# A feed-forward in four 64x64 quadrants of the TensorE array, with the lower rows one product behind the upper

## The chip, the cores and the metric

The kernel runs on one core of one Trainium2 chip. The metric is device time of one execution in microseconds (us), median of several runs. The span that a profile gives, from the first to the last instruction, is about 1.9 us shorter than the timed run (392.3 against 394.16 us before).

## The reference

Sigmoid attention, then a feed-forward with SiLU. Cut to what matters:

```python
q, k, v: (8 batches, 12 heads, 448, 64)         # float32
scores = q @ k.T / sqrt(64) - log(448)
attn   = sigmoid(scores) @ v                    # (8, 12, 448, 64)
x      = attn.transpose(0, 2, 1, 3).reshape(3584, 768)
h      = x @ w_in                               # w_in (768, 2048)
g      = h * sigmoid(h)
out    = g @ w_out                              # w_out (2048, 768)
```

## The kernel before

The kernel works in float16. A unit is 4 heads of one batch, so there are 24 units. The attention products S (scores) and V (values) contract over 64 and give 64 rows. They already run in the four 64x64 quadrants of the array, four matmuls at a time (in the trace three of a group start 3 to 4 ns behind the one before, and the V groups of 448 columns follow each other every 189 ns):

```python
def v_matmuls(pt, n, slots, N):
    for c in range(NCH):
        for h in range(2):              # rows 0-63 or 64-127 of the array
            for j in range(2):          # columns 0-63 or 64-127
                ck = NCH * j + c
                nc.tensor.matmul(
                    pt[64 * j : 64 * j + 64, h, :N],
                    v16[n % NV][64 * h : 64 * h + 64, j, c * D : (c + 1) * D],
                    at[64 * h : 64 * h + 64, slots[ck // 2], ck % 2, :N],
                    start=(c == 0), stop=(c == NCH - 1), skip_group_check=True,
                )
```

The feed-forward uses the whole 128x128 array. Its first product (G1) is this; the second (G2) has the same form, 384 columns wide, in a seven-product scheme of which only the count matters here (14 pairs of output blocks, 7 products of 8 matmuls each):

```python
def piece(self):                        # G1: one or two blocks of 128 hidden units
    # ... (cut)
    def go(z, fc):
        for cc in range(NCC):           # 6 blocks of the contraction
            nc.tensor.matmul(
                bank[:, z * N : z * N + N], wi[:, cc, fc * P : (fc + 1) * P], x[:, cc, c0:c1],
                start=(cc == 0 and z == 0), stop=(cc == NCC - 1), skip_group_check=True,
            )
    # ... (cut)
```

For the first two batches G1 is done in two "narrow" parts, of 256 and of 192 columns, so that it can begin early; later batches use 448 columns. Attention steps are set between feed-forward products. A plan in Python decides the order; in the compiled program the order on each engine is fixed. The inputs are loaded by GpSimd-issued DMA, 224 KB per load of queries, keys or values of one unit, up to 384 KB for `w_in` and 768 KB for `w_out` (the figures in the code are the plan's own estimates, and no argument here rests on them):

```python
def load(key, deps, fn, nd, size):
    first = [("issue", pl.loads)] if pl.loads else []
    pl.loads += 1
    pl.op("POOL", 650, key, deps + first, fn, nbytes=nd / 16 * (21 + 0.0368 * size))
```

## Time and profile before

| | before |
|---|---|
| median time | 394.16 us (3 runs) |
| span in the profile | 392.3 us |
| TensorE busy | 98% |
| changes of form, 76 to 329 us | 144, each about 98 ns |
| TensorE instructions in the program, waits not counted | 7,448 |

The list of what TensorE waited for (us in total, times, longest), kernel before:

```profile
PE gm L355 <- DMA xq<-in_q_dram: 1.4, 1, 1.4
PE gm L841 <- DVE warm L195: 1.2, 1, 1.2
PE gm L346 <- DMA xk<-in_k_dram: 0.8, 1, 0.8
PE gm L579 <- DVE xt L830: 0.3, 1, 0.3
PE att L407 <- ACT at L812: 0.2, 1, 0.2
```

The timeline of TensorE, kernel before (start in us, duration in us, group). Eighteen matmuls of the whole array are 18 x 189.2 ns = 3.41 us by their spacing, and two groups of four quadrants 0.38 us. A round (131.46 to 135.47) takes 4.01 us, so two changes of form cost 0.22 us.

```profile
131.46 0.57 PE L407 MATMUL att<-qT,kT 64*64 64x448 f16 x8
131.96 3.58 PE L579 MATMUL gm<-xt,wi 128*128 128x448 f16 x18
135.47 0.57 PE L407 MATMUL att<-qT,kT 64*64 64x448 f16 x8
```

### The profile page before, as it was taken

How to read it: one execution, taken by the hardware profiler on the slowest of the kernel's cores; microseconds unless marked ns; L12 is line 12 of the kernel's file. 1: busy time of each engine (PE TensorE's matmuls, PEld its weight loads, DVE VectorE, ACT ScalarE, POOL GpSimd, SP SyncE). 2: the span in 40 equal slices, each digit the busy share in tenths (PEclk: the TensorE clock that was granted, in tenths of full speed). 3: DMA queues.
4: the chain of work that ended last, by engine and by line, in shares of the span. 5: the costliest groups of instructions: out<-in, count | busy, mean ns of one | idle time of the engine just before them, and what ended most of it. 6: DMA issues, size and time to landing. Idle time of an engine off the chain costs nothing.

```text
span 392.3 us, 8872 instructions
## 1 busy us (share of the span) xinstructions
PE 383.0 (98%) x3723; PEld 210.2 (54%) x3723; DVE 199.7 (51%) x326; ACT 222.7 (57%) x332; POOL 65.0 (17%) x97
## 2 busy tenths in 40 slices
PE   6999999999999999999999999999999999999995
PEld 2567777775454455444454444444554445555562
DVE  1444788545455444554546345545554445554552
ACT  1876787487556855567645875686554772144110
POOL 9655322502222021020120120000000000000000
PEclk8999999999999999999999999999999999999998
DMA  7999999999999786993487877632023001320333
GB/s 105 199 209 203 210 208 203 164 143 145 158 192 196 105 137 116 179 165 74 73 149 174 149 123 99 107 71 52 21 62 82 0 2 34 82 48 2 70 81 91
DMA packets 80599, 45.93 MB, mean 117 GB/s; under 512 B 50608, under 2 KB 79792, under 8 KB 80560
## 3 DMA queue, kind: packets, MB, share of 16 engines
q0 software_dynamic: 25008, 22.81, 39.9%
q1 hardware_dynamic: 55552, 22.56, 31.9%
q8 instruction: 29, 0.48, 0.5%
q14 instruction: 10, 0.08, 0.1%
HBM read 45.61 MB, written 11.01 MB: 144 GB/s over the span
## 4 chain that ended last, share of the span: by engine, by line
PE 93%; DVE 2%; DMA 1%; ACT 1%; issue 1%; POOL 0%; ACTq 0%; POOLq 0%; DVEq 0%
PE gm L579 37%; PE gm L665 34%; PE att L407 11%; PE att L419 8%; PE gm L355 1%; DMA xq<-in_q_dram 1%; PE gm L856 1%; ACT at L812 1%; PE gm L346 1%; DVE gs L272 0%; DVE gt L542 0%; DVE xt L830 0%; ACT sg L537 0%; DVE qT L376 0%; DVE wo L272 0%
## 5 line engine op out<-in xcount | busy, mean ns | idle before, releaser
L579 PE MATMUL gm<-xt,wi 128*128 128x448 f16 (+2 forms) x960 | 158.4, 316 | 0.4 <-DVE xt L830 0.3
L451 ACT ACTIVATE at<-att 128x896 f16<-128x896 f32 x126 | 109.6, 916 | 52.5 <-PE att L407 52.5
L542 DVE TENSOR_TENSOR gt<-gm,sg 128x448 f16<-128x448 f32 (+2 forms) x128 | 79.8, 624 | 90.7 <-ACT sg L537 90.5
L579 PEld LDWEIGHTS <-wi 128*128 128x128 f16 x960 | 86.0, 98 | 66.4 <-issue 14.9
L537 ACT ACTIVATE sg<-gm 128x448 f16<-128x448 f32 (+2 forms) x128 | 70.1, 548 | 53.7 <-PE gm L579 49.0
L679 DVE SCALAR_TENSOR_TENSOR us<-gm,us 128x384 f32<-128x384 f32 x70 | 38.7, 553 | 46.5 <-PE gm L665 31.4
L665 PE MATMUL gm<-wo,gt 128*128 128x384 f16 x336 | 61.3, 327 | 0.0
L665 PEld LDWEIGHTS <-gt 128*128 128x128 f16 x448 | 42.0, 98 | 34.2 <-issue 7.9
L407 PE MATMUL att<-qT,kT 64*64 64x448 f16 (+2 forms) x840 | 53.8, 325 | 0.6 <-ACT at L812 0.2
L812 ACT ACTIVATE at<-att 128x1024 f16<-128x1024 f32 (+3 forms) x48 | 37.7, 826 | 15.2 <-PE att L407 15.0
L665 PEld LDWEIGHTS <-gs 128*128 128x128 f16 x336 | 31.6, 98 | 25.4 <-issue 5.7
L235 POOL DMA_DIRECT2D v<-in_v_dram x24 | 17.4, 725 | 138.3 <-PE att L407 122.5
L665 PE MATMUL gm<-so,gs 128*128 128x384 f16 x224 | 40.3, 327 | 0.0
L419 PE MATMUL att<-at,v 64*64 64x448 f16 (+2 forms) x840 | 37.6, 314 | 0.1
L686 ACT ACTIVATE us<-gm 128x384 f32<-128x384 f32 x28 | 13.8, 493 | 40.7 <-PE gm L665 39.6
L407 PEld LDWEIGHTS <-kT 64*64 64x64 f16 x840 | 17.7, 106 | 27.8 <-issue 23.2
L419 PEld LDWEIGHTS <-v 64*64 64x64 f16 x840 | 21.2, 106 | 13.6 <-issue 6.8
L461 DVE TENSOR_SCALAR xt<-att 128x896 f16<-128x896 f32 x18 | 19.6, 1091 | 11.4 <-PE att L419 11.4
L224 POOL DMA_DIRECT2D xq<-in_q_dram x27 | 19.8, 735 | 15.4 <-issue 5.8
L665 PE MATMUL gm<-wo,gs 128*128 128x384 f16 x112 | 21.0, 326 | 0.0
L665 PE MATMUL gm<-so,gt 128*128 128x384 f16 x112 | 21.0, 326 | 0.0
L215 POOL DMA_DIRECT2D xk<-in_k_dram x24 | 17.5, 727 | 15.8 <-PE gm L346 8.9
(32 smaller groups left out, 114.6 us busy)
## 6 DMA issues: line engine op xcount, KB each, us to landing
out_dram<-us SPq DMA_DIRECT2D x112, 96.0 KB, 2.2
xk<-in_k_dram POOLq DMA_DIRECT2D x24, 224.0 KB, 7.2
v<-in_v_dram POOLq DMA_DIRECT2D x24, 224.0 KB, 6.6
xq<-in_q_dram POOLq DMA_DIRECT2D x21, 224.0 KB, 8.5
wo<-in_moe_w_out_dram POOLq DMA_DIRECT2D x4, 768.0 KB, 15.3
wi<-in_moe_w_in_dram POOLq DMA_DIRECT2D x8, 192.0 KB, 7.5
wi<-in_moe_w_in_dram POOLq DMA_DIRECT2D x4, 384.0 KB, 9.7
qT<-xq SPq DMA_TRANSPOSE x32, 3.8
```

Source lines behind the costliest of these rows:

```text
L215: lambda: nc.gpsimd.dma_start(xk[n % NX].rearrange("p (j c) -> p j c", j=2), src(k, b, g)),
L224: lambda: nc.gpsimd.dma_start(xq[n % NX][:, D : D + 2 * S].rearrange("p (j c) -> p j c", j=2)[:, :, lo:hi], src(q, b, g)[:, :, lo:hi],),
L407: nc.tensor.matmul(pt[64 * h : 64 * h + 64, r, lo : lo + (c1 - c0) * D], kT[n % NTR][64 * r : 64 * r + 64, i, 64 * h : 64 * h + 64], qT[n ...
L419: nc.tensor.matmul(pt[64 * j : 64 * j + 64, h, :N], v16[n % NV][64 * h : 64 * h + 64, j, c * D : (c + 1) * D], at[64 * h : 64 * h + 64, sl ...
L451: lambda: nc.scalar.activation(at[:, sl], pt[:, :, :S], AF.Sigmoid, bias=NEG_LOG_S, scale=QKSCALE),
L461: lambda: nc.vector.tensor_scalar_mul(x[:, 2 * g : 2 * g + 2, :], pt[:, :, :S], SX), prio=-2,
L537: lambda: nc.scalar.activation(t[:, :ncol], src_, AF.Sigmoid, scale=ISX), prio=0,
L542: lambda: nc.vector.tensor_tensor(o, src_.rearrange("p (a t) -> p a t", a=nb), t[:, :ncol].rearrange("p (a t) -> p a t", a=nb), ALU.mult),
L579: nc.tensor.matmul(bank[:, z * N : z * N + N], wi[:, cc, fc * P : (fc + 1) * P], x[:, cc, c0:c1], start=(cc == 0 and z == 0), stop=(cc == ...
L665: nc.tensor.matmul(bank[:, :HE], lhs[:, c, :], rhs[:, c, :], start=first and c == 0, stop=(c == HFC - 1), skip_group_check=True,)
L679: lambda: nc.vector.scalar_tensor_tensor(o, bank[:, :HE], ISX, u, ALU.mult, ALU.add), prio=-2,
L812: lambda: nc.scalar.activation(at[:, base : base + m, :, :N], src_, AF.Sigmoid, bias=NEG_LOG_S, scale=QKSCALE),
```

## The change

The intent: run everything in quadrants, so that the array never changes its form. Each feed-forward matmul becomes four. The upper rows (h = 0) and the lower rows (h = 1) of one product add into the same bank of PSUM, where this kernel's matmuls write their results. The plan keeps the two from being in it at once, which I took to be needed. So the lower rows work on a product whose upper rows ended at least 450 ns earlier, and a semaphore makes TensorE wait for its own earlier matmul. Transposes become quadrant matmuls against the identity, and all PSUM tiles become single banks, so attention evictions are split in two. The core of the diff (the rest, on the plan's order, banks and evictions, is cut):

```diff
-            def go(z, fc):
-                for cc in range(NCC):
-                    nc.tensor.matmul(
-                        bank[:, z * N : z * N + N], wi[:, cc, fc * P : (fc + 1) * P], x[:, cc, c0:c1],
-                        start=(cc == 0 and z == 0), stop=(cc == NCC - 1), skip_group_check=True,
-                    )
+            def mm(h, c):
+                z, cc = divmod(c, NCC)
+                f0 = fcs[z] * P
+                return [
+                    nc.tensor.matmul(
+                        bank[64 * j : 64 * j + 64, z * N : z * N + N],
+                        wi[64 * h : 64 * h + 64, cc, f0 + 64 * j : f0 + 64 * j + 64],
+                        x[64 * h : 64 * h + 64, cc, c0:c1],
+                        start=(c == 0 and h == 0), stop=(h == 1 and cc == NCC - 1), skip_group_check=True,
+                    )
+                    for j in range(2)
+                ]
...
+    def lower_ready():
+        if not fifo:
+            return False
+        q, c = fifo[0]
+        return c > 0 or (q.left is not None and pl.t >= q.left + 450.0)
+
+    def lane_step(p=None, c=0):
+        low = fifo.popleft() if lower_ready() else None
+        ...
+        def go():
+            if p:
+                p.last = p.mm(0, c)[-1]
+            if low:
+                if low[1] == 0:
+                    wait = nc.tensor.nop()
+                    left = low[0].last
+                ins = low[0].mm(1, low[1])
+                if low[1] == 0:
+                    for a_, b_ in ((wait, left), (ins[0], wait)):
+                        tc.add_manual_dep(
+                            a_.ins, b_.ins.name,
+                            mybir.DependencyInfo(mybir.DependencyClass.Sync, mybir.DependencyReason.DATA),
+                            reason="the upper rows have left the bank",
+                        )
```

G2 is changed in the same way, with 384 columns. The compiled program has 18,338 TensorE instructions instead of 7,448, and 226 waits of TensorE on itself.

## The prediction

> **What bounds the kernel now.** TensorE. The page shows PE busy 98% of the 392.3 us span, the waits of TensorE sum to about 4 us (all at the start), and the chain of waits is 93% PE. So what fills that busy time? From the starts of successive matmuls (timeline): 128x448 products follow each other every 189 ns; four 64x64 matmuls of 448 columns start 3 to 4 ns apart, and such a group also takes 189 ns; 384 columns take 162.5 ns. Feed-forward work at these rates is 273 us (960 + 784 matmuls), attention 64 us. The rest:

> - Changes between the 128x128 and the 64x64 form. From 76 to 329 us I count 144, each adding about 98 ns to the normal spacing: 14.1 us. Before 76 us there are 98 more, with 13 us (some of it waits for data). [...]
> - Transposes: 56 + 112 groups at 56 ns, 9.4 us. Filler matmuls on zeros, start and tail: about 5 us each.

> **What the change removes.** All mode changes (about 23 us clean), and about 6 us of transposes (112 groups of four small matmuls, estimated at 29 ns each, instead of 168 at 56).

> **What it adds.** Four times as many feed-forward matmuls of a quarter of the size: the same array work if both halves are full. The build order shows where they aren't: 58 steps with the upper half alone, 58 with the lower alone (14 us, half of it wasted: 7 us), and some 500 steps that pair a 448- with a 384-column product and last as long as the wider (7 us wasted). By counts times measured spacing, feed-forward is 287 us instead of 273. ScalarE evictions are split by bank: 916 ns becomes 2 x 548, +23 us, about 66% busy overall, but near 90% before 76 us, where it and the loads (DMA full from 10 to 68 us) hold back part of the gain.

> **Rate of the quadrants.** The attention products already run four quadrants at full rate, with weight loads of 106 ns hidden (even at 192 columns: 82.5 ns per group). I expect the feed-forward to do the same. [...]

> **The wait on itself.** 226 waits, one per product, each placed at least 450 ns after the upper rows' last matmul. That matmul lasts 349 ns in the trace, so the semaphore should already be there: under 25 ns each, mostly nothing.

> **Sum.** First stage ends near 70 us instead of 76. After it: 255.5 us feed-forward, 47.7 us attention, 5 us tail, 2 us of stalls: span about 380, time about 381.5 us (timed runs lie 1.9 us over the span).

> Predicted 381.5 us, 80% range 373 to 391. Faster by over 2%: 0.69; within 2%: 0.23; slower: 0.08.

> **Right if** groups start every 189 and 162 ns throughout, no 98 ns steps remain, waits of TensorE on TensorE sum to a few us, ScalarE is near 250 us busy, and attention visits cost just their 189 ns per group.

> **Wrong if** TensorE cannot be fed: 18,338 instructions instead of 7,448 mean about 20 ns each, and no stretch before shows more than one matmul per 50 ns for long; then groups are over 189 ns apart and time may rise far above 394. Or if each self-wait costs 100 ns or more (+20 us). Or if late loads, ScalarE or full banks show as new waits of TensorE in the first 80 us.

The 7 us for steps with one half alone are counted from the build order that has the lag. The 29 ns for a group of four transposes are an estimate that can be worked out from the trace of before: 82.5 ns at 192 columns and 189.2 ns at 448 are 26.7 ns for each 64 columns and 2.5 ns beside. In the changed kernel they took 31 to 32 ns.

## More of the kernel before

From the page of the kernel before: its first lines, three rows of the table in 40 slices of 9.8 us (busy tenths; PEclk is the granted clock of TensorE in tenths; DMA is the mean busy share of the 16 DMA engines), and the row of the DMA queue that brings instructions (packets, MB, share of the 16 engines' span).

```profile
span 392.3 us, 8872 instructions
...
PE 383.0 (98%) x3723; PEld 210.2 (54%) x3723; DVE 199.7 (51%) x326; ACT 222.7 (57%) x332; POOL 65.0 (17%) x97
...
PE   6999999999999999999999999999999999999995
...
PEclk8999999999999999999999999999999999999998
DMA  7999999999999786993487877632023001320333
...
q8 instruction: 29, 0.48, 0.5%
```

TensorE is full all the way (98%), its clock is up (0.993 on average; at half only from 7.8 to 11.2 us), and DMA is full from the second slice to the thirteenth (10 to 127 us, 186 GB/s). The line of q8 looks harmless, and the prediction did not use it. Read with the count after the change (below), it says that TensorE's program comes in packets of 0.48 MB / 29 = 16 KB while the kernel runs (29 packets for 7,448 instructions, and 72 for 18,338 after the change: one for about 256).

## The result, and the profile after

The changed kernel is slower: median 415.65 us (414.08 to 417.07, 4 runs) against 393.99 us (4 runs). The ratio is 1.0547, with a 95% interval of 1.0496 to 1.0599. Ratios are computed as the mean time of one kernel's runs over that of the other's in the same rounds, so they are not quite the ratio of the medians quoted. Results are correct in this and in every run below.

The same parts of the page, kernel after (a slice is 10.4 us):

```profile
span 415.2 us, 20334 instructions
...
PE 376.3 (91%) x9168; PEld 322.7 (78%) x9168; DVE 203.6 (49%) x376; ACT 234.6 (56%) x506; POOL 65.0 (16%) x97
...
PE   7769667885699989999999999999999999999995
...
PEclk9996888999899999999999999999999999999999
DMA  8999995399449994969868999654413101220234
...
q8 instruction: 72, 1.18, 1.2%
```

TensorE has holes in the first third and is as full as before afterwards. In the same stretch its clock drops: the trace shows it at half for 20.4 us in five spells between 32 and 114 us, one of 6.8 us and four of 3.4 us. In them a group of 256 columns mostly takes 213 ns instead of 109, and one of 192 columns 160 ns instead of 83. The list of TensorE's waits, kernel after (all lines of over 0.4 us):

```profile
PE ps L666 <- issue: 25.0, 15, 3.0
PE ps L765 <- issue: 2.4, 3, 0.9
PE ps L451 <- issue: 1.4, 1, 1.4
PE ps L493 <- DVE qT L465: 1.3, 4, 0.6
PE ps L947 <- DVE warm L195: 1.2, 1, 1.2
PE ps L451 <- DMA xk<-in_k_dram: 0.9, 1, 0.9
PE ps L493 <- DVE xt L936: 0.6, 2, 0.3
PE ps L666 <- DVE xt L936: 0.5, 1, 0.5
```

"issue" means that the engine waited for nothing that the profile shows: no semaphore, no buffer, no other engine. It is 29 us in 19 gaps, and there was none before. The timeline of TensorE shows two such gaps whole, kernel after:

```profile
40.42 0.56 PE L666 MATMUL ps<-xt,wi 64*64 64x256 f16 x10
42.80 2.05 PE L666 MATMUL ps<-xt,wi 64*64 64x256 f16 x67 [1.83 <-issue]
...
45.98 0.52 PE L666 MATMUL ps<-xt,wi 64*64 64x256 f16 x12
48.76 1.58 PE L666 MATMUL ps<-xt,wi 64*64 64x256 f16 x34 [2.26 <-issue]
```

```
kernel  block  entered  pause just  fetch in it     fetch   next block  length of
        at no. at, us   before, us  starts after    took    entered at  the block
before   1217   41.50     0.11        2.07 us       0.97     48.48        6.98
before   1473   48.48     0.08        2.79          0.97     55.29        6.81
before   4033  161.01     0.00        0.53          0.89    177.15       16.14
after     961   24.72     1.39        3.58          0.89     30.78        6.06
after    1473   36.77     0.03        3.63          0.95     42.80        6.03
after    1729   42.80     2.10        3.67          0.94     48.76        5.96
after    1985   48.76     2.53        4.19          0.94     55.38        6.62
after    2241   55.38     2.16        3.75          0.97     61.55        6.17
after    2753   67.80     1.85        1.64          0.95     71.63        3.83
after    9409  207.68     0.15        1.54          0.89    213.28        5.60
```

(The pause is start to start, so it includes a normal spacing. Block 4033 has a second fetch, 14.65 us after its start.) While DMA is full (205 GB/s from 20 to 67 us), a block of the changed kernel lasts about 6.1 us (5.90 to 6.62): about 3.7 us until the fetch begins, 0.95 us for the fetch, and about 1.4 us from its landing to the next block's first instruction (1.25 to 1.60). The kernel before took 6.27 us or more for every block, and it has no pause. (In its quiet stretch this link is not seen: a fetch begun at 208.57 us landed 0.87 us after the next block had been entered, without a pause. So how far ahead of TensorE a fetch must land is not settled for that stretch.) The changed kernel has 18,338 instructions for 7,448, at the same spacing of the groups, and would use up a block of narrow products in an estimated 2.6 to 3.5 us: 32 groups (four weight loads and four matmuls each) at the measured 82.5 to 109 ns. After 67 us the fetch starts sooner (1.64 and 1.05 us after entry) and the blocks get shorter at once (3.83 and 3.59 us). But they do not get short enough: from 67.8 to 71.6 us DMA moved only 6 GB/s, and the block still lasted 3.83 us, with a pause of 1.16 us behind it. So narrow products in quadrants used up a block too soon here even beside a nearly idle DMA; beside a full one the pauses are more and longer (eight of 1.4 to 2.9 us between 18 and 68 us).

The pauses of over 0.3 us at block ends sum to 34.6 us in the changed kernel (20 of them; one after 200 us, at 399 us, where DMA is light; that one is not explained) and to nothing in the kernel before. Where the loss lies is seen from the start of the last narrow G1 matmul: at 90.4 us before, at 118.8 us after. From there to the end the kernel before takes 301.9 us and the changed one 296.4 us. All of the loss, and more, falls before that point: 28.4 us, and the pauses before it sum to 28.6 us. (That the two agree so closely is partly chance: the half-clock spells fell there too, and the quadrant transposes saved an estimated 5.8 us, from 168 groups at 56 ns before and 112 at 32 ns after.)

The speed of the quadrants is as predicted. From 202 to 398 us, 4,399 times a matmul and the fourth one behind it were compared: the spacing is 188 to 190 ns or 162 to 163 ns in most of them, and over 200 ns in 88.

### The profile page after: what moved, and what is told of

It reads as the page before. It is cut to its first block, busy times and chain, and to the rows that moved or that the text cites. A ratio compares the mean times of both kernels' runs of the same rounds, so it can differ in the third digit from the quotient of the medians.

```text
span 415.2 us, 20334 instructions
## 1 busy us (share of the span) xinstructions
PE 376.3 (91%) x9168; PEld 322.7 (78%) x9168; DVE 203.6 (49%) x376; ACT 234.6 (56%) x506; POOL 65.0 (16%) x97
## 4 chain that ended last, share of the span: by engine, by line
PE 88%; issue 7%; DVE 2%; DMA 1%; POOL 0%; ACT 0%; POOLq 0%
PE ps L666 39%; PE ps L765 31%; PE ps L493 8%; PE ps L505 8%; PE ps L451 1%; DMA xq<-in_q_dram 1%; DVE kT L465 1%; DVE qT L465 1%; PE ps L947 0%; DVE so L272 0%; DVE xt L936 0%; ACT at L914 0%; DVE wo L272 0%; POOL xk L215 0%; DVE us L779 0%
## 5 line engine op out<-in xcount | busy, mean ns | idle before, releaser
L666 PE MATMUL ps<-xt,wi 64*64 64x448 f16 (+2 forms) x3840 | 229.6, 323 | 25.5 <-issue 25.0
L666 PEld LDWEIGHTS <-wi 64*64 64x64 f16 x3840 | 161.4, 112 | 46.0 <-issue 30.3
L536 ACT ACTIVATE at<-ps 128x448 f16<-128x448 f32 x252 | 122.4, 547 | 46.0 <-PE ps L493 41.4
L615 DVE TENSOR_TENSOR gt<-ps,sg 128x448 f16<-128x448 f32 (+2 forms) x128 | 78.1, 622 | 97.1 <-ACT sg L610 96.8
L610 ACT ACTIVATE sg<-ps 128x448 f16<-128x448 f32 (+2 forms) x128 | 69.7, 550 | 75.3 <-PE ps L666 71.3
L765 PE MATMUL ps<-wo,gt 64*64 64x384 f16 x1344 | 109.8, 323 | 0.0
L765 PEld LDWEIGHTS <-gt 64*64 64x64 f16 x1792 | 98.6, 107 | 8.7 <-issue 0.6
L765 PEld LDWEIGHTS <-gs 64*64 64x64 f16 x1344 | 79.2, 107 | 11.8 <-issue 3.7
L765 PE MATMUL ps<-so,gs 64*64 64x384 f16 x896 | 84.7, 323 | 1.5 <-issue 1.5
L493 PE MATMUL ps<-qT,kT 64*64 64x448 f16 (+2 forms) x840 | 80.4, 320 | 2.4 <-DVE qT L465 1.3
L786 ACT ACTIVATE us<-ps 128x384 f32<-128x384 f32 x28 | 13.8, 495 | 32.4 <-PE ps L765 30.9
## 6 DMA issues: line engine op xcount, KB each, us to landing
wi<-in_moe_w_in_dram POOLq DMA_DIRECT2D x4, 384.0 KB, 9.6
```

The source lines that it names most:

```text
L493: nc.tensor.matmul(pt[r][64 * h : 64 * h + 64, lo : lo + (c1 - c0) * D], kT[n % NTR][64 * r : 64 * r + 64, i, 64 * h : 64 * h + 64], qT[n ...
L536: lambda r=r: nc.scalar.activation(at[:, sl, r], pt[r][:, :S], AF.Sigmoid, bias=NEG_LOG_S, scale=QKSCALE),
L610: lambda: nc.scalar.activation(t[:, :ncol], src_, AF.Sigmoid, scale=ISX), prio=0,
L615: lambda: nc.vector.tensor_tensor(o, src_.rearrange("p (a t) -> p a t", a=nb), t[:, :ncol].rearrange("p (a t) -> p a t", a=nb), ALU.mult),
L666: nc.tensor.matmul(bank[64 * j : 64 * j + 64, z * N : z * N + N], wi[64 * h : 64 * h + 64, cc, f0 + 64 * j : f0 + 64 * j + 64], x[64 * h : ...
L765: nc.tensor.matmul(bank[64 * j : 64 * j + 64, :HE], lhs[64 * h : 64 * h + 64, c, 64 * j : 64 * j + 64], rhs[64 * h : 64 * h + 64, c, :], s ...
```

## The experiments

Theory A: TensorE runs out of instructions at block ends, because the fetch of the next block is held up while DMA is full of data loads. Theory B: the waits of TensorE on itself cost the time. Both were suppositions until the runs; that the fetch queues behind the data, as some expectations put it, was not shown (few3). Other rivals were that a quadrant feed-forward is slow in itself, and that late buffers hold it.

### lag900: twice the lag

```diff
-        return c > 0 or (q.left is not None and pl.t >= q.left + 450.0)
+        return c > 0 or (q.left is not None and pl.t >= q.left + 900.0)
...
-            pl.t = max(pl.t, q.left + 450.0)
+            pl.t = max(pl.t, q.left + 900.0)
```

> The changed kernel with the lower rows at least 900 ns behind the end of the upper rows instead of 450. Theory A (instruction blocks: TensorE runs out of instructions at every 256th, because the fetch of the next 16 KB block queues behind the data loads): nothing changes in the count of instructions or the loads, so 411 to 420 us, with pauses at the same instruction numbers 193 + 256k and a sum of 28 to 36 us. Theory B (the waits of TensorE on itself cost the time): with the semaphore long there, the lost 20 to 30 us come back, under 400 us.

Measured: 418.58 us (415.82 to 421.98, 4 runs), ratio to before 1.0576 (1.0524 to 1.0629). Pauses at 193 + 256k sum to 34.0 us, and in the stretch of full DMA blocks last 5.75 to 6.20 us. The edit also changes the order of the plan. Theory B expected under 400 us, and it falls.

### cols: twice the instructions in the kernel before, no quadrant feed-forward

In the kernel before, each feed-forward matmul of 128 columns is cut into its left and its right half. The array runs the two side by side, as the time shows: one after the other they would double the 273 us of feed-forward work, and the runs took 396.19 and 399.84 us. The edit:

```diff
                 for cc in range(NCC):
-                    nc.tensor.matmul(
-                        bank[:, z * N : z * N + N], wi[:, cc, fc * P : (fc + 1) * P], x[:, cc, c0:c1],
-                        start=(cc == 0 and z == 0), stop=(cc == NCC - 1), skip_group_check=True,
-                    )
+                    for j in range(2):
+                        nc.tensor.matmul(
+                            bank[64 * j : 64 * j + 64, z * N : z * N + N], wi[:, cc, fc * P + 64 * j : fc * P + 64 * j + 64], x[:, cc, c0:c1],
+                            start=(cc == 0 and z == 0), stop=(cc == NCC - 1), skip_group_check=True,
+                        )
```

(G2 in the same way.)

> The kernel before, with each feed-forward matmul of 128 columns cut in two of 64 (left and right half of the array at once): twice its instructions, the same array time, no lag and no wait of TensorE on itself, all changes of form kept. Theory A: in the first 76 us a block of 256 instructions would last about 5.1 us, under the 6.0 to 6.3 us that a fetch takes there, so pauses of about 1 us appear at every 256th instruction; 5 to 12 us are added before 76 us, little after (400 to 407 us). Theory B: 394 us, no such pauses.

Measured: 396.19 and 399.84 us; ratio 1.0079 (1.0011 to 1.0147). Five pauses of 0.4 to 2.1 us, 4.4 us together, stand at numbers 1729, 1985, 2241, 2497 and 3265, which are 193 + 256k again; the blocks between lasted 5.92 to 6.19 us. There is neither a lag nor a self-wait in this kernel, and its clock was not at half from 3.9 to 396.4 us, so these pauses came without a dropped clock. The loss is smaller than I expected, since only five blocks were used up before the next had come, and at 2% it counts as the same time; but the signature is there without any part of the lag scheme.

### traffic and before_traffic: more DMA where it was light

Both kernels get 48 more loads into spare tiles that nothing reads, four behind each of the loads of units 12 to 23. TensorE's program stays the same, instruction for instruction, in both.

```diff
+    spare = [sb(f"spare{i}", [2, S], F16) for i in range(4)]
+    extra = [0]
+
+    def load_spare(n):
+        b, g = divmod(n, NQ)
+        z = extra[0] % 4
+        extra[0] += 1
+        nc.gpsimd.dma_start(spare[z], src(v, b, g))
...
         load_v(n)
+        if n >= 12:
+            for z in range(4):
+                pl.op("POOL", 650, ("spare", n, z), [("v", n)], lambda n=n: load_spare(n))
```

> The changed kernel with 48 more loads of values into spare tiles that nothing reads, four behind each of the loads of units 12 to 23: DMA stays busy where it was light. Instructions of TensorE are the same. Theory A: after 200 us, where the changed kernel had two pauses at block ends, new ones of 0.3 to 2 us appear at instruction numbers 193 + 256k, wherever DMA is full; 5 to 20 us longer, with DMA share over 0.9 there. Theory B: no new pauses; only waits for late data, if any, which would be at the attention products and not at block ends.

> The kernel before with the same 48 extra loads. Theory A: here a block of 256 instructions lasts 14 to 16 us after 100 us, far over what a fetch takes even in a full queue, so no pause at block ends; the time stays within 394 to 400 us, and what is added is waits for late data. If instead TensorE is 30 us or more late here too, the extra loads hurt by themselves and the run with them says nothing of the fetch.

Measured, one look each: the changed kernel with the loads takes 455.56 us, the kernel before with the same loads 395.11 us (before alone in those rounds: medians 394.54 and 394.31 us). From the page of the changed kernel with the extra loads (a slice is 11.3 us):

```profile
PE   6977768967995979697998997875999999999986
...
PEclk9888879998998889999999999996999999999999
DMA  8999992695499999999999999999752300230134
```

From the page of the kernel before with the extra loads (9.8 us a slice):

```profile
PE   7998999999999999999999999999999999999995
...
PEclk9999999999999999999999999999999999999998
DMA  8999999999999999999999999999953001320333
```

DMA is now full from 125 to 318 us in the first and until 285 us in the second. In the changed kernel the holes of TensorE follow: 31 pauses at block ends, 64.3 us, up to 6.7 us long. The list of TensorE's waits in that run is led by these lines:

```profile
PE ps L677 <- issue: 36.7, 17, 6.4
PE ps L776 <- issue: 11.8, 10, 2.8
PE ps L505 <- issue: 5.9, 2, 5.4
```

The kernel before, under the same load, has no pause at all, because its blocks last 13.8 to 23 us after 100 us. This pair shows theory A most directly: the program of TensorE did not change, only the traffic beside it. The changed kernel lost 40 us, twice the 20 us that I had put as the limit. (The expectation's "two pauses after 200 us" in the changed kernel are one, at 399 us; another is at 196 us.)

### few3: only three loads under way

In the changed kernel each load waits for the landing of the third load before it:

```diff
+        issue = fn
+
+        def fn():
+            d = issue()
+            if len(landed) >= 3:
+                tc.add_manual_dep(
+                    d.ins, landed[-3].ins.name,
+                    mybir.DependencyInfo(mybir.DependencyClass.Sync, mybir.DependencyReason.DATA),
+                    reason="few loads under way",
+                )
+            landed.append(d)
```

> The changed kernel, with each load of data waiting for the landing of the third load before it, so that 3 are under way instead of up to 8. Theory A: the instruction fetch queues behind fewer bytes; its delay from entering a block to its start falls from about 3.7 us to 1.5 to 2.5 us before 68 us, blocks there last 4 to 5 us instead of 6.0 to 6.2, the sum of pauses falls from 34 us to under 20, and the time to 395 to 407 us (if the loads keep up). Theory B: no change, 413 to 418 us.

Measured: 424.49 us (423.11 to 427.18, 4 runs), ratio 1.0757 (1.0708 to 1.0807). A miss. The pauses fell to 24.8 us, and between 42 and 50 us the fetch did start 1.2 and 1.7 us after its block was entered; but between 53 and 75 us it was again 3.5 to 4.2 us, there partly beside the large loads of `w_out`, with DMA at 207 GB/s. Meanwhile the loads came later, TensorE waited 4.6 us for `w_in`, and the clock was lower (0.955 on average, against 0.974). So the fetch's delay is not simply the number of loads under way. How the DMA engines order a fetch among data is left open.

### hyb1: whole array while DMA is full, quadrants afterwards

In the changed kernel a product can also run in the whole array. Here the first two batches' G1 does, before anything else of the feed-forward:

```diff
+    F1, F2 = 2, 0
+    whole = [True]
...
+        whole[0] = p.full is not None
         ff_wait(deps)
+        if p.full:
+            while fifo:
+                drain_one()
+            each = 6 if p.N != HE else 4
+            for c in range(p.n):
+                d = p.N / 2.4 + 2.5
+                pl.pe(d, p.key if c == p.n - 1 else None, [], lambda: p.full(c))
+                pl.main += d
+                if (c + 1) % each == 0 or c == p.n - 1:
+                    between()
+            return
...
+            def mm_full(c):
+                z, cc = divmod(c, NCC)
+                f0 = fcs[z] * P
+                nc.tensor.matmul(
+                    bank[:, z * N : z * N + N], wi[:, cc, f0 : f0 + P], x[:, cc, c0:c1],
+                    start=(c == 0), stop=(cc == NCC - 1), skip_group_check=True,
+                )
+
+            if b < F1:
+                p.full = mm_full
```

(Beside it, the plan counts 190 ns for the changes of form, and takes two attention steps at a time, while products are whole; G2 gets the same choice by `pi < F2`.)

> The changed kernel, but the feed-forward products of the first two batches (384 matmuls in the first 76 us) again in the whole 128x128 array; all else in quadrants. It has 2,280 fewer instructions where DMA is full. Theory A: the pauses before 70 us vanish, the first stage ends at 73 to 77 us as in the kernel before, the clock stays up, a few pauses of up to 2 us stay between 76 and 200 us: 386 to 396 us. Theory B (self-waits): 158 of 226 remain, so at most a third of the loss returns: 405 to 412 us.

Measured: **384.0 us** (382.47 to 384.74, 4 runs), ratio to before **0.9737** (0.9711 to 0.9763). It beats both kernels, and it is a little better than the 386 to 396 us expected. (The count of self-waits in that expectation was wrong: 194 of 226 remain in this program, which speaks the more against theory B.) From its page (9.6 us a slice), and its list of waits of TensorE down to 1 us:

```profile
PE   7898999998999999999999999999999999999995
...
PEclk9999999999999999999999999999999999999998
DMA  8999999999999696994679999725132002400334
```

```profile
PE ps L798 <- issue: 2.0, 3, 1.1
PE ps L703 <- DMA wi<-in_moe_w_in_dram: 1.9, 2, 1.6
PE ps L990 <- DVE warm L195: 1.2, 1, 1.2
PE ps L496 <- DVE qT L468: 1.0, 2, 0.6
```

The pauses are down from 34.6 to 4.5 us, the clock stays up until the end (0.996 on average), and DMA is as full in the first slices as ever. About half of what is left of the pauses comes just after the switch to quadrants, at 93 and 99 us (1.5 and 0.75 us).

### hyb2: quadrants from the fourth batch only

As hyb1, with `F1, F2 = 3, 2`: the third batch and the first two pairs of output blocks are whole, too.

> As hyb1, and the third batch and the first two pairs of output blocks in the whole array too, so that quadrants begin near 137 us, where DMA becomes lighter. Theory A: sum of pauses under 5 us; changes of form return between 76 and 137 us (+5 us against hyb1) and about 6 us of pauses go: 384 to 394 us. If it is over 400 us, something else in the quadrants costs time.

Measured: 388.65 us (388.48 to 389.2, 4 runs), ratio 0.9864 (0.9846 to 0.9882), inside the range; but I had expected it level with hyb1 or just better, and it is 4.65 us slower. Its pauses sum to 5.2 us, so waiting longer gained nothing there, and 39 changes of form after the last narrow product cost an estimated 3.8 us, at the 98 ns of the kernel before. Of the two switching points tried, the earlier is the better.

### rev: the mirror of hyb1

Quadrants in the first two batches, the whole array in all later products:

```diff
-    F1, F2 = 2, 0
+    F1, F2 = 2, 99
...
-            if b < F1:
+            if b >= F1:
```

> The mirror of hyb1: the first two batches' feed-forward in quadrants, all later feed-forward products in the whole array, so the changes of form return there and no lower row lags after the first stage. Theory A: the loss of the changed kernel lies in the first two batches alone; the pauses of its first stage stay (the last narrow product starts at 105 to 120 us instead of 84 to 90), the rest takes 300 to 306 us as in the kernel before: 408 to 424 us in all, pauses at block ends only in the first 120 us. Theory B: 68 of 226 self-waits remain, so most of the loss is gone: 394 to 402 us.

Measured: 422.9 us (422.3 to 424.45, 4 runs), ratio 1.0738 (1.071 to 1.0766). Pauses at block ends sum to 28.3 us, all before 114 us. (The self-waits left are 32, not 68 as the expectation says; theory B would then have nearly all of the loss gone.) With it the four combinations are complete; times in us from the four traces:

| first two batches' G1 | later products | last narrow G1 matmul starts at | from there to the end | span |
|---|---|---|---|---|
| whole (before) | whole | 90.4 | 301.9 | 392.3 |
| whole (hyb1) | quadrants | 83.7 | 298.3 | 382.1 |
| quadrants (after) | quadrants | 118.8 | 296.4 | 415.2 |
| quadrants (rev) | whole | 116.5 | 304.4 | 420.9 |

The first part is long exactly where the narrow products run in quadrants; the rest is 3.6 us (first part whole) or 8.0 us (first part in quadrants) shorter where quadrants follow. (The two parts are not quite the same work in each row, since attention steps shift a little between them; the spans are.)

Two cautions on hyb1. Compared with before, 44 attention matmuls of 448 columns have moved behind the mark, an estimated 2.1 us at their spacing of 189 ns for four. With them, quadrants in the later products gain about 5.7 us, and the spans of rev and after differ by the same 5.7 us. The other 4.5 us of hyb1's 10.2 us come in the first part, where its G1 is whole, as in before. There it has 69 changes of form against 106 (attention steps are taken two at a time) and quadrant transposes. So not all of hyb1's gain is the gain of a quadrant feed-forward; how the 4.5 us divide was not tested.

## Why the prediction was wrong

The prediction was 381.5 us, with a range of 373 to 391; the changed kernel takes 415.65 us, outside it and in the wrong direction.

- **Bound by TensorE, changes of form at 98 ns, their sum: right.** They are gone in the changed kernel (every matmul in its trace is 64*64). hyb1, which keeps the quadrants for most of the feed-forward, gains 10.2 us of span over before, about 5.7 us of it by the quadrants there. The prediction had 6 us for the part after its first stage (316 us before, 310 after).
- **Rate of the quadrants once fed: right.** The groups are 189 and 162 to 163 ns apart after 202 us, with twice the instructions.
- **Self-waits mostly nothing: right.** None shows in the list of waits, lag900 gains nothing, and 194 of them fit into 384.0 us.
- **The step that failed** is "First stage ends near 70 us instead of 76", with "2 us of stalls" for the whole kernel. (In the trace of before, 76.06 us is where the attention products become 448 columns wide. In the changed kernel that is at 100.4 us, 24.4 us later instead of some 6 us earlier; by the last narrow product it is 28.4 us later. From 100.4 us to the end it takes 314.8 us, 11.3 us of them pauses, where the sum had 310: that part was about right.) It carried the 82.5 ns of short bursts of attention over to a long stretch of narrow products, without asking where the instructions come from. In the runs 256 TensorE instructions took about 6.1 us while DMA was full (5.90 to 6.62 us in the changed kernel, 5.75 to 6.20 in lag900, 5.92 to 6.19 in cols): 34.6 us of pauses in place of the 2 us, and half-clock spells of 20.4 us. The pauses (which include a normal spacing of 0.1 to 0.2 us each), less the allowed 2 us, are already 32.6 of the 35.2 us between the predicted span (380) and the measured one (415.2). The clock's own share was not separated from them, but the two overlap: block 1217, which ran at half clock from 32.1 us to its end, lasted 6.0 us like its neighbours, with a pause of 0.03 us behind it.
- **"Wrong if TensorE cannot be fed" named the right danger in the wrong form.** It looked for groups spaced wider throughout. In truth the groups keep their spacing at full clock (109 and 83 ns for the narrow ones, 189 and 162 to 163 ns later), and up to 3.2 us at a time are missing at block ends, nearly all of it where DMA is busy. It also was not put into the sum, though its size could be read. In the trace of before, up to 76 us, fetches start 1.95 to 3.3 us after their block is entered and take 0.95 us. That is an estimated 2.9 to 4.2 us at least for 256 instructions, against 2.6 to 3.5 us of narrow quadrant work, so pauses were to be expected from the trace alone.
- **ScalarE near 250 us busy: too high.** It is 234.6 us. That the loads hold back the first stage shows only slightly in hyb1 (1.9 us of waits for `w_in`); that ScalarE does was not tested.

Shown are: that the pauses stand at block ends (every kernel), that they need many instructions per time (cols, before_traffic) and that a busy DMA makes them many and long (traffic; the changed kernel's own quiet two thirds agree, but their wider products also make a block last mostly 5 to 6 us; one pause of 1.16 us came with DMA nearly idle), and that without most of them quadrants in the later products gain (hyb1, by about 5.7 us). Not settled is the route by which data loads delay the fetch (few3).

## What to carry to other kernels

Cutting matmuls into quadrants multiplies instructions (18,338 for 7,448 here), and instructions are loaded too (72 packets of 16 KB for 29, one for 256 of TensorE's): before such a change, divide 256 by the instructions per us that the new program will use, and compare it with the time from entering a block to its fetch's landing in the old trace, in the stretch where DMA is busiest. That time was only a lower bound here: it read 2.9 to 4.2 us, and the blocks of the changed kernel then lasted about 6.1 us. A gap that the profile blames on nothing ("issue"), at a regular instruction number, was the sign of it here (193 + 256k). A change can be right in one stage and wrong in another, so try it by stage: here quadrants after the narrow products, with the changes of hyb1's plan, give 0.974 of the time, and quadrants everywhere 1.055.
